# Head of the tensor queue, the order of the first nine pairs, and the partitions of one add, in an attention and mixture-of-experts kernel

## The chip, the cores and the metric

The kernel runs on one core of a Trainium2 chip. Times are device microseconds of that core; the kernel's time is the median of several executions, and one further execution was recorded by the hardware profiler.

## What is computed

Two attentions follow each other. The first has 8 batches of 8 heads over 576 positions of width 64, with a bias from a running sum. Its output, 8 batches of 576 rows of 512, goes through four experts, each a one-head attention of its own with projections in and out; a gate picks two experts per row.

```python
scores = scale * np.matmul(q, k.transpose(0, 1, 3, 2))
cum = np.cumsum(np.maximum(s, 0.0), axis=-1)
bias = -(cum[:, :, :, None] - cum[:, :, None, :])
scores = np.where(causal, -1e9, scores + np.minimum(bias, 0.0))
attn = softmax(scores)                      # less the row maximum, sum + 1e-9
x = np.matmul(attn, v)                      # heads side by side: B, S, 512
logits = x @ w_gate                         # the two largest of four weigh the experts
for e in range(4):                          # causal softmax attention per expert
    a = softmax(where(causal, -1e9, scale * (x @ wq[e]) @ (x @ wk[e]).T))
    out += gate[e] * (a @ (x @ wv[e])) @ wo[e]
```

## The kernel before, in words

The unit of work is a pair of heads, or of experts. Fifty pairs follow each other: pairs 0 to 7 are the heads of the first two batches, 8 and 9 the experts of batch 0, then four head pairs and two expert pairs by turns. Each of the five engines works through its own queue in the order in which the program issues to it. That order is written out by hand in the string `STEPS`: a step `n:x` issues the step x of slot n, and each engine takes its steps in the order of the string. Slots begin at -2, since a pair's preparation begins two slots ahead. The steps used below are these.

- `h0` to `h3` (ScalarE) round the queries and keys of pair n+2 to their high parts; `hc` (a DMA) brings its running sums; `l0`, `l1` and on (VectorE, on GpSimd for pair 1) form the low parts of pair n+1, and `lq`, `lk` copy its high parts.
- `m0` to `m5` (TensorE) form products whose row maximum is wanted, `m0` to `m2` for pair n+2 and `m3` to `m5` for pair n+1, each in a PSUM bank; `M0` to `M5` (VectorE) reduce a bank and give it back. `mt` (TensorE) turns the maxima of pair n+1 from columns into rows, `mA` (ScalarE) negates and `mq` (two DMAs) writes them beside the queries. All this stands ahead of the pair's scores.
- `s0` to `s6` (TensorE, lines 674 and 679) are the scores of pair n, each in a bank; `E0` to `E6` (ScalarE, line 695) take the exponent and give the bank back; `d0` to `d3` (GpSimd) clear the triangle and add the row sums up in the tile `r` (`d1` at lines 755 and 756, `d3` at line 766).
- `v0` to `v7` (TensorE, line 832) multiply by the values of pair n-1, `V0` and `V1` copy out. `n0`, `n1` (VectorE, line 949) scale two pairs by the reciprocal sums, which `r0` to `r4` bring through DMAs; `N` and `o` split the result in high and low parts.
- `ld` (a DMA) loads queries and keys of pair n+3 into one of three `raw` tiles; `lv` loads values; `w` loads weights, into the tiles that the reciprocals use too.
- `z0` to `z47` (TensorE, line 1273) are dummy products of 64 columns that put TensorE to work between others; ahead of all stands a loop of `FIRST_IDLE` dummy products. Each shows as two records in the trace.

A bank is taken by a step on TensorE from the one given back longest ago, so the order of steps also sets whose release a product waits for. With eight banks, in the order before `10:s5` takes the bank that `10:M4` gives back, and on VectorE `10:M4` stands right behind `9:n0`. From slot 10 on the string is the same in both orders, and seven of its lines in slots 6 to 8 are too.

Of the kernel before, what the change touches and what calls it, by code (L numbers as in the profile page):

```python
# [40 lines left out]
FIRST_IDLE, IDLE = 12, 48  # L41
# [28 lines left out]
def heads(t, at, c0, c1):  # L70
# [17 lines left out]
    "-2:h3 -1:lq -2:h1 -1:lk -2:z0 -2:z1 -2:z2 -2:h0 -2:z3 -1:l1 0:lq -2:z4 -2:z5 -1:ld -2:hc -2:z6 "  # L88
    "-1:cu -2:h2 -2:m1 -1:m5 -1:h0 -1:l0 -2:m2 -2:z7 -1:f1 -1:h3 0:h2 0:h0 -2:M1 -2:M2 -2:z8 -2:z9 "
    "0:f2 -1:hc -1:m3 -1:h2 -1:M5 -2:m0 -1:h1 0:hc -2:z10 -2:z11 -1:M3 0:h3 -1:m4 0:m4 -2:M0 -1:M4 "  # L90
    "-1:m0 -1:M0 -1:m2 -1:M2 -2:z12 -1:mt -1:mA -1:mq -2:z13 0:h1 -1:m1 -1:M1 0:m5 0:m3 0:M5 0:m0 "
    "-2:z14 -2:z15 -2:z16 -2:z17 -2:z18 0:l0 0:lk 0:s4 0:E4 0:M4 0:s2 0:M3 0:s1 0:E1 0:s5 0:l1 0:mt "
    "0:mA 0:s6 0:M0 0:ld 0:s3 0:s0 0:E5 -2:z19 0:m2 1:l0 0:E2 0:mq 0:E3 0:E0 1:m3 1:m4 -2:z20 -2:z21 "
    "-2:z22 1:hc 1:h2 1:h3 0:d1 0:d0 1:lq 0:E6 0:m1 1:m5 1:M3 1:M5 -2:z23 0:d3 1:h1 1:s5 1:s3 1:E3 "
    "1:s4 1:h0 0:M1 1:s1 1:s2 1:s0 1:E5 0:M2 1:s6 0:lv 1:E2 -2:z24 1:ld 1:v3 1:E4 0:d2 1:d2 1:v4 1:M4 "
    "2:m3 0:e0 2:lq 1:lk 1:E1 1:E0 1:m0 1:M0 0:lc -2:z25 1:v5 1:v6 -2:z26 1:mt 1:lv 1:mA 2:M3 2:h0 "
    "2:lv 1:l1 -2:z27 2:m4 1:m2 1:M2 2:m5 1:m1 1:v7 1:V1 -2:z28 -2:z29 0:b0 1:mq 0:B0 1:v0 1:v1 1:d1 "
    "2:M5 1:v2 2:M4 1:M1 2:lk -2:z30 2:h3 -2:z31 1:d0 2:h2 1:e0 2:hc 2:s1 2:E1 2:s6 2:E6 2:d3 2:mt "
    "2:l0 2:s3 2:mA 2:ld 2:s5 2:h1 2:s2 2:s0 1:E6 2:E3 2:E2 2:s4 2:E4 3:h2 2:v0 2:l1 3:l0 -2:z32 "
    "-2:z33 1:w0 2:m2 3:m5 2:E5 1:d3 3:M5 2:v1 -2:z34 -2:z35 2:M2 2:v2 2:V0 -2:z36 2:E0 2:w0 -2:z37 "  # L100
    "1:b0 3:m3 -2:z38 3:m4 1:B0 3:ld 3:M3 2:m1 1:V0 3:h1 2:v3 2:v4 2:v5 2:mq 2:v6 2:M1 3:h0 2:v7 3:w0 "
    "2:V1 2:m0 3:s1 3:s0 3:hc 3:E1 2:d0 3:h3 3:s6 3:E6 3:s2 3:r0 3:E0 2:M0 2:d1 3:M4 3:s4 3:s3 3:s5 "
    "3:mt -2:z39 2:d2 2:e0 4:m3 3:lk 3:d0 4:m5 -2:z40 -2:z41 -2:z42 -2:z43 3:r1 4:M5 -2:z44 3:E5 "
    "-2:z45 3:m2 3:E2 4:m4 3:E3 4:w1 4:h3 3:d1 3:E4 3:d3 4:M3 3:e0 4:h0 3:M2 3:d2 -2:z46 3:v0 3:v1 "
    "3:v2 3:m0 2:b0 3:b0 3:mA 4:lk 2:B0 4:M4 3:l1 3:r2 4:lv 3:V0 3:r4 3:m1 3:v3 3:v4 3:lq 4:l0 3:B0 "
    "4:h1 3:n1 4:h2 3:v5 3:mq 3:v6 3:v7 3:M1 4:s1 4:E1 4:hc 3:r3 4:s0 4:E0 3:n0 5:r0 4:s5 4:s3 4:E3 "
    "3:M0 4:s2 4:s4 4:d0 4:E5 4:mt 4:mA -2:z47 5:r1 4:s6 4:l1 4:E6 5:m5 4:E2 3:lv 4:m0 -2:zz 5:m4 "
    "4:M0 4:m2 4:v3 3:V1 4:m1 4:E4 5:w0 4:w0 4:d1 4:v4 4:v5 4:ld 4:v6 4:M2 4:v7 4:lq 4:V1 3:N1 5:r2 "
    "4:e0 5:h1 4:v0 4:v1 5:v3 5:v4 5:h0 4:v2 5:v0 5:v1 4:d2 4:d3 5:v2 5:M5 5:m3 5:hc 4:V0 5:M4 5:h2 "
    "5:M3 4:mq 5:s6 5:r3 5:s0 5:h3 5:V0 5:E6 5:s5 3:N0 5:s3 3:o1 4:M1 3:o0 5:s2 5:s4 5:E3 5:s1 5:E0 "  # L110
    "5:r4 5:E4 7:ld 5:E1 5:mt 5:n0 5:lq 6:m5 5:E5 5:v5 5:v6 5:n1 5:v7 5:m1 5:mA 5:m2 6:m4 5:N0 5:V1 "
# [9 lines left out]
    "8:E3 8:n0 8:l1 8:s0 8:s4 8:mt 8:g1 8:g2 8:g3 8:E2 8:s6 8:mA 9:l0 8:h2 8:ld 7:d2 8:a0 8:E0 8:hc "  # L121
    "7:d3 8:a1 7:v5 8:v3 8:A1 7:v6 7:v2 8:N0 8:A0 8:s1 8:E4 8:l2 8:E1 8:s5 8:E5 9:t0 9:T0 9:m3 9:h2 "
    "9:l2 8:d0 9:h0 9:m5 7:v7 8:v0 8:v1 8:v4 8:v5 8:v6 8:mq 8:m0 9:r0 9:M3 9:r1 9:r2 9:m4 9:M5 8:m2 "
    "9:h3 8:d1 7:V0 8:m1 9:lk 8:E6 8:v7 8:e0 8:M0 8:V1 8:v2 9:s0 9:s5 8:V0 9:s1 8:M1 9:h1 8:d2 9:s2 "
    "9:E0 7:V1 8:M2 9:M4 9:t1 9:s4 9:hc 9:s3 9:mt 9:E5 9:s6 9:E1 9:E4 8:o0 8:N1 9:mA 9:E3 9:l1 10:m5 "
    "9:v0 9:E2 9:v1 9:v2 9:V0 9:E6 9:m1 9:m2 9:r4 10:h2 9:d0 9:lq 9:n1 9:m0 9:r3 8:d3 10:M5 10:lq "
    "9:l3 10:m4 10:m3 9:n0 9:mq 9:T1 9:td 10:h0 9:d1 10:v0 10:v1 9:v3 10:M4 9:v4 10:V0 9:v5 9:v6 9:v7 "
    "10:lv 9:N0 10:ld 9:V1 9:M0 10:s2 10:s5 10:s3 8:o1 10:E2 9:o0 10:E5 10:s0 9:N1 10:E3 10:s4 10:s6 "
    "9:M1 10:s1 9:o1 10:M3 9:d2 10:E4 10:p2 9:M2 10:h3 10:P2 10:p0 10:p1 10:h1 10:mt 10:lk 10:E0 "
    "10:l2 10:E1 10:l3 9:d3 10:hc 10:a1 10:a0 10:d1 10:P0 10:A1 10:d2 10:mA 10:A0 10:d0 10:m0 11:hc "  # L130
    "11:lk 10:l1 10:m2 11:m3 10:m1 10:l0 11:m4 10:v2 10:v3 10:v4 10:v5 11:h3 10:M2 11:r0 10:P1 10:mq "
# [1250 lines left out]
```

## Time and profile before

| | us |
|---|---|
| median of 3 runs | 663.42 (662.9 to 664.12) |
| the profiled execution | 663.8 |
| its span on the core | 662.1 |
| TensorE busy | 650.7 |
| VectorE busy | 558.2 |
| ScalarE busy | 450.3 |
| GpSimd busy | 424.4 |

The span runs from the first to the last instruction; 1.7 us of the profiled time lie around it. TensorE counts as busy while a dummy product runs, and while it runs at half clock; the granted clock is shown apart.

### The profile page before, as it was taken

To read this page: it belongs to the slowest core of one execution; us is meant where nothing else is said; L and a number is where in the kernel's file an instruction comes from. 1 tells how busy PE (TensorE), PEld (TensorE's weight loads), DVE (VectorE), ACT (ScalarE), POOL (GpSimd) and SP (SyncE) were. 2 spreads that over 40 slices of the span, in tenths; PEclk is the share of its full clock that TensorE was granted. 3 is DMA by queue.
4 is the path that set the end of the run, shared out by engine and by line. 5 is a ranking of instruction groups with operands and counts; after the bars stand their busy time and mean duration, and the time that the engine had idled before them with its cause. 6 is when DMAs were issued, how large, how long until landed. Compare 5 with 4: busy or idle time off the path is not lost.

```text
span 662.1 us, 16453 instructions
## 1 busy us (share of the span) xinstructions
PE 650.7 (98%) x5976; PEld 547.3 (83%) x5976; DVE 558.2 (84%) x1432; ACT 450.3 (68%) x980; POOL 424.4 (64%) x530
## 2 busy tenths in 40 slices
PE   8999999999999999999999999999999999999997
PEld 5888798888897888888888878978888889779885
DVE  8687978997989889898989989897998986781995
ACT  5488867766668766776667776677676757556464
POOL 8576566678667576667776586585766765837030
PEclk8699999989999999999999999999999999999999
DMA  4253552553554463535633545445535443331323
GB/s 145 64 165 113 163 140 64 143 143 92 154 141 119 130 165 82 139 121 151 176 93 110 174 119 158 128 123 142 158 84 142 139 120 97 99 106 37 93 65 111
DMA packets 52286, 81.22 MB, mean 123 GB/s; under 512 B 18430, under 2 KB 26622, under 8 KB 52206
## 3 DMA queue, kind: packets, MB, share of 16 engines
q1 hardware_dynamic: 52206, 80.18, 44.5%
q8 instruction: 47, 0.77, 0.5%
q14 instruction: 33, 0.27, 0.1%
HBM read 44.55 MB, written 10.09 MB: 83 GB/s over the span
## 4 chain that ended last, share of the span: by engine, by line
PE 81%; DVE 7%; DMA 4%; ACT 3%; issue 2%; SPq 1%; DVEq 0%; ACTq 0%
PE pvp L832 16%; PE pq L1058 12%; PE s L674 11%; PE s L679 10%; PE pw L1058 9%; PE mx L613 9%; PE po L1058 7%; PE sm L882 3%; DVE mx L627 3%; PE idle L1273 1%; DMA rb<-rr 1%; ACT p L695 1%; DVE pv L949 1%; DMA raw<-in_qk_dram 1%; PE po L1034 1%
## 5 line engine op out<-in xcount | busy, mean ns | idle before, releaser
L627 DVE CUSTOM_DVE_ANT_0 mx<-mx,mask 128x64 f32<-128x64 f32 (+7 forms) x432 | 185.0, 445 | 38.9 <-PE mx L613 24.5
L695 ACT ACTIVATE p<-s 128x512 f32<-128x512 f32 x288 | 161.5, 593 | 64.3 <-PE s L679 63.3
L715 POOL TENSOR_SCALAR_AFFINE_SELECT p<-p 64x128 f32<-64x128 f32 (+2 forms) x183 | 111.7, 611 | 117.8 <-ACT p L695 103.2
L674 PE MATMUL s<-q,k 128*128 128x320 f32 (+3 forms) x672 | 173.5, 288 | 2.3 <-DVE mcol L627 2.2
L679 PE MATMUL s<-q,k 97*128 97x320 f32 (+3 forms) x672 | 163.8, 285 | 0.6 <-DMA q<-mr 0.6
L674 PEld LDWEIGHTS s<-q,k 128*128 128x128 f32 (+1 forms) x672 | 125.4, 187 | 8.3 <-issue 1.9
L679 PEld LDWEIGHTS s<-q,k 97*128 97x128 f32 (+1 forms) x672 | 124.6, 187 | 2.2 <-DMA q<-mr 1.0
L761 POOL TENSOR_TENSOR r<-r,p 128x640 f32<-128x640 f32 x84 | 118.0, 1405 | 6.8
L587 DVE TENSOR_TENSOR q<-raw,q 64x576 fp32r<-64x576 f32 (+1 forms) x86 | 82.8, 971 | 25.7 <-ACT q L547 11.9
L832 PE MATMUL pvp<-p,v 128*64 128x192 f32 (+4 forms) x1024 | 102.2, 334 | 0.8 <-DVE mcol L627 0.8
L613 PE MATMUL mx<-k,q 96*64 96x448 bf16 (+6 forms) x960 | 92.6, 300 | 1.8 <-DMA k<-p 0.9
L832 PEld LDWEIGHTS pvp<-p,v 128*64 128x64 f32 x1024 | 66.8, 136 | 28.4 <-ACT p L695 2.5
L592 DVE TENSOR_TENSOR k<-raw,k 64x576 fp32r<-64x576 f32 (+1 forms) x86 | 87.1, 1020 | 2.6 <-ACT k L578 0.3
L1058 PE MATMUL pq<-xh,wqkh 128*128 128x288 f32 x256 | 77.7, 304 | 0.3 <-ACT pv L846 0.3
L1058 PE MATMUL pq<-xl,wqkh 128*128 128x288 f32 x256 | 75.5, 295 | 0.0
L1058 PE MATMUL pq<-xh,wqkl 128*128 128x288 f32 x256 | 75.5, 295 | 0.0
L550 ACT ACTIVATE k<-raw 64x576 fp32r<-64x576 f32 x96 | 64.6, 681 | 7.5 <-DMA raw<-in_qk_dram 5.7
L613 PEld LDWEIGHTS <-q 96*64 96x64 bf16 x960 | 46.6, 111 | 27.0 <-issue 10.0
L627 DVE DVE_READ_ACCUMULATOR2_ANT mcol<- 128x1 f32 x480 | 65.9, 137 | 0.7
L547 ACT ACTIVATE q<-raw 64x576 fp32r<-64x576 f32 x96 | 64.2, 678 | 1.1
L755 POOL TENSOR_TENSOR r<-p 128x256 f32<-128x256 f32 x37 | 28.9, 780 | 52.6 <-ACT p L695 52.1
L846 ACT ACTIVATE pv<-pvp 128x320 f32<-128x320 f32 (+1 forms) x92 | 36.4, 405 | 27.5 <-PE pvp L832 27.4
(151 smaller groups left out, 1249.3 us busy)
## 6 DMA issues: line engine op xcount, KB each, us to landing
raw<-in_qk_dram SPq DMA_DIRECT2D x30, 576.0 KB
rb<-rr SPq DMA_DIRECT2D x92, 144.0 KB
q<-q SPq DMA_DIRECT2D x45, 288.0 KB
k<-k SPq DMA_DIRECT2D x39, 288.0 KB
v<-in_vm_dram SPq DMA_DIRECT2D x32, 256.0 KB
out_dram<-o SPq DMA_DIRECT2D x32, 256.0 KB
q<-mr SPq DMA_DIRECT2D x96, 2.2 KB
raw<-in_qk_dram SPq DMA_DIRECT2D x4, 288.0 KB
```

The lines of the kernel that those rows point to most:

```text
L550: nc.scalar.activation(k2[0:64, j], get_raw(n, j)[64:128], AF.Copy)
L587: eng.tensor_tensor(a[64:128, j], get_raw(n, j)[0:64], q2[0:64, j].bitcast(F32), op=OP.subtract)
L592: eng.tensor_tensor(c[0:64, j], get_raw(n, j)[64:128], c[64:128, j].bitcast(F32), op=OP.subtract)
L613: nc.tensor.matmul(t[64 * j : 64 * j + 64, c0 : c0 + k1 - k0], q2[0:RC, 64 * qt : 64 * qt + 64], k2[0:RC, k0:k1], start=True, stop=True,)
L627: nc.vector.tensor_tensor_reduce(t[:, c0 : c0 + w], t[:, c0 : c0 + w], mask[:, m0 : m0 + w], scale=1.0, scalar=mcol[n][:, 9:10] if slot == ...
L674: nc.tensor.matmul(t[0:nk, c0 : c0 + q1 - q0], K1[r1(n)][:, j, k0 : k0 + nk], Q1[r1(n)][:, j, q0:q1], start=True, stop=False,)
L679: nc.tensor.matmul(t[0:nk, c0 : c0 + q1 - q0], K2[r2(n)][0 : RM + 1, j, k0 : k0 + nk], Q2[r2(n)][0 : RM + 1, j, q0:q1], start=False, stop= ...
L695: nc.scalar.activation(heads(ptile[n], PCHUNK[ci], 0, 512)[:, x % 2], tl[x], AF.Exp, scale=0.125)
L715: nc.gpsimd.affine_select(out=a, in_=a, pattern=[[0, a.shape[1]], [1, w]], compare_op=OP.is_ge, fill=0.0, base=0, channel_multiplier=-1,)
L761: add(r[:, :, q0:S], r[:, :, q0:S], chunk_of(2, c, c + S - q0), op=OP.add)
L832: nc.tensor.matmul(cur[h][64 * j : 64 * j + 64, q0 - PVC[h] : q1 - PVC[h]], vsl(j, kt), heads(ptile[n], at, c, c + q1 - q0)[:, j], start=f ...
L1058: nc.tensor.matmul(t[0:nk, 0:w], l, r, start=(x == 0), stop=(x == len(terms) - 1))
```

## The change

1. The loop at the head issues 32 dummy products of 128 columns in place of 12 of 256.
2. The steps of slots -2 to 6 and of slots 8 to 10 are put in another order. No step is added or left out, 779 places of the string lie between the first and the last that differ.
3. In the last step of a pair's sums, `d3`, the add on GpSimd takes 128 partitions in place of 64; the triangle is still cleared in 64. The other 64 rows of its second operand hold zeros.

The diff, with the lines of `STEPS` cut to the parts spoken of below:

```diff
-FIRST_IDLE, IDLE = 12, 48
+FIRST_IDLE, IDLE = 32, 48
...
-    "-2:h3 -1:lq -2:h1 -1:lk -2:z0 -2:z1 -2:z2 -2:h0 -2:z3 -1:l1 0:lq -2:z4 -2:z5 -1:ld -2:hc -2:z6 "
-    "-1:cu -2:h2 -2:m1 -1:m5 -1:h0 -1:l0 -2:m2 -2:z7 -1:f1 -1:h3 0:h2 0:h0 -2:M1 -2:M2 -2:z8 -2:z9 "
-    "0:f2 -1:hc -1:m3 -1:h2 -1:M5 -2:m0 -1:h1 0:hc -2:z10 -2:z11 -1:M3 0:h3 -1:m4 0:m4 -2:M0 -1:M4 "
-    "-1:m0 -1:M0 -1:m2 -1:M2 -2:z12 -1:mt -1:mA -1:mq -2:z13 0:h1 -1:m1 -1:M1 0:m5 0:m3 0:M5 0:m0 "
-    "-2:z14 -2:z15 -2:z16 -2:z17 -2:z18 0:l0 0:lk 0:s4 0:E4 0:M4 0:s2 0:M3 0:s1 0:E1 0:s5 0:l1 0:mt "
-    "0:mA 0:s6 0:M0 0:ld 0:s3 0:s0 0:E5 -2:z19 0:m2 1:l0 0:E2 0:mq 0:E3 0:E0 1:m3 1:m4 -2:z20 -2:z21 "
-    "-2:z22 1:hc 1:h2 1:h3 0:d1 0:d0 1:lq 0:E6 0:m1 1:m5 1:M3 1:M5 -2:z23 0:d3 1:h1 1:s5 1:s3 1:E3 "
...
-    "4:M0 4:m2 4:v3 3:V1 4:m1 4:E4 5:w0 4:w0 4:d1 4:v4 4:v5 4:ld 4:v6 4:M2 4:v7 4:lq 4:V1 3:N1 5:r2 "
...
+    "-1:ld -2:h0 -2:h3 -2:z0 -2:hc -2:h2 -1:h0 -2:z1 -1:l0 -2:h1 -1:lk -1:l1 -2:z2 -2:z3 -2:z4 -1:lq "
+    "-1:m3 0:h2 0:lk -1:M3 -2:m0 0:lq -2:m2 -1:h2 -1:h1 -2:m1 -1:m5 -1:m4 -2:M0 -2:z5 -2:z6 -2:z7 "
+    "-1:cu -1:f1 -1:h3 -2:z8 -2:z9 -2:z10 -2:M1 -2:z11 0:h0 -2:z12 -2:z13 -2:z14 -1:hc 0:m4 0:f2 "
+    "-1:m1 -1:m2 -2:M2 -1:M5 -1:M4 0:h1 -1:mt -1:mA -2:z15 -1:M1 0:m3 0:h3 0:hc 0:m5 0:M3 -2:z16 "
+    "-1:m0 0:M5 1:m4 0:m2 -2:z17 -2:z18 -1:M0 -1:mq 0:s0 0:E0 -1:M2 0:ld 0:s4 0:E4 0:s3 0:E3 0:s1 "
+    "0:l1 0:l0 -2:z19 0:M4 0:M2 0:s6 0:mt 0:mA 0:E1 0:s2 0:mq 0:E2 0:s5 0:E6 1:m5 0:E5 0:m1 1:M5 1:h3 "
+    "0:m0 1:h2 1:m3 1:hc 0:d1 1:M3 0:lv -2:z20 -2:z21 -2:z22 -2:z23 2:lv 1:s0 1:E0 1:s6 1:s5 1:M4 "
+    "1:E6 0:M1 1:s1 0:M0 1:s2 1:h1 1:s3 1:ld 0:d3 0:d0 1:h0 1:E1 1:E2 1:s4 1:mt 2:m5 2:hc 1:m1 1:v0 "
+    "1:l0 1:E4 2:M5 0:d2 2:lq 1:v1 0:e0 -2:z24 -2:z25 1:mA -2:z26 -2:z27 1:E3 1:m2 -2:z28 1:lk 2:h0 "
...
+    "4:s3 4:s4 4:E1 4:E2 4:s5 4:s0 4:E3 4:lq 4:lk 4:mt 4:s6 4:l1 4:m1 4:E5 3:o1 5:lv 5:m5 4:E0 4:E6 "
+    "4:ld 4:mA 5:r0 5:r1 4:m2 3:N0 4:E4 5:m4 5:M5 5:m3 4:M2 4:v0 4:v3 4:v1 4:v2 5:M3 4:v4 5:h1 4:v5 "
+    "5:h2 5:v3 5:M4 4:w0 4:d0 5:r2 4:v6 5:v0 4:M1 4:v7 5:v1 4:d1 5:v4 4:e0 4:V1 7:ld 4:d2 5:v2 5:V0 "
...
-    "9:v0 9:E2 9:v1 9:v2 9:V0 9:E6 9:m1 9:m2 9:r4 10:h2 9:d0 9:lq 9:n1 9:m0 9:r3 8:d3 10:M5 10:lq "
-    "9:l3 10:m4 10:m3 9:n0 9:mq 9:T1 9:td 10:h0 9:d1 10:v0 10:v1 9:v3 10:M4 9:v4 10:V0 9:v5 9:v6 9:v7 "
-    "10:lv 9:N0 10:ld 9:V1 9:M0 10:s2 10:s5 10:s3 8:o1 10:E2 9:o0 10:E5 10:s0 9:N1 10:E3 10:s4 10:s6 "
+    "9:v4 9:v5 10:m5 9:m1 9:l0 9:n0 9:r4 9:v6 9:T1 10:h1 9:v0 9:v1 10:lk 9:E6 8:o1 9:v2 9:N0 10:M5 "
+    "10:v0 10:hc 9:E4 9:E5 10:v1 8:e0 9:V0 9:v7 9:l3 10:V0 9:E3 10:m4 9:m2 9:d1 9:n1 10:h3 9:V1 10:m3 "
+    "10:M3 9:d2 9:M2 9:m0 9:N1 9:o0 9:o1 9:mq 9:d3 10:s0 10:s4 10:E4 10:lq 10:s2 10:lv 10:E2 10:E0 "
+    "10:M4 10:s1 10:E1 9:M1 10:s3 10:p2 10:h2 10:p1 10:p0 9:M0 10:ld 10:h0 10:E3 10:s5 10:l2 10:E5 "
...
-                a = heads(p, PTAIL, 0, 64)[0:64]
-                lower(a, 64)
+                a = heads(p, PTAIL, 0, 64)
+                lower(a[0:64], 64)
                 if n >= SUMMED:
-                    nc.gpsimd.tensor_tensor(r[0:64, :, 512:S], r[0:64, :, 512:S], a, op=OP.add)
+                    nc.gpsimd.tensor_tensor(r[:, :, 512:S], r[:, :, 512:S], a, op=OP.add)
...
     for k in range(FIRST_IDLE):
-        idle(0, 256)
+        idle(0, 128)
```

## Rows read from the trace of the kernel before

**Rows 1.** The page, part 1: busy time, share and instructions of each engine.
```profile
PE 650.7 (98%) x5976; PEld 547.3 (83%) x5976; DVE 558.2 (84%) x1432; ACT 450.3 (68%) x980; POOL 424.4 (64%) x530
```

**Rows 2.** Windows: stretch, length, busy (count) PE, PEld, DVE, ACT, POOL; PEclk, DMA share, GB/s.
```profile
84.60:139.40 54.80, 54.80 (x526) 47.43 (x526) 46.66 (x123) 39.35 (x88) 38.58 (x40) 1.00 0.47 120
139.40:146.00 6.60, 5.05 (x29) 4.88 (x29) 6.53 (x14) 3.66 (x7) 5.65 (x6) 0.74 0.72 177
...
200.00:300.00 100.00, 99.68 (x935) 83.23 (x928) 90.40 (x235) 71.95 (x157) 71.52 (x86) 1.00 0.47 129
```

**Rows 3.** Windows, short ones around the changes of the granted clock.
```profile
12.20:12.40 0.20, 0.20 (x9) 0.16 (x4) 0.00 (x0) 0.20 (x1) 0.20 (x1) 0.82 0.99 219
...
29.40:29.60 0.20, 0.20 (x3) 0.19 (x2) 0.19 (x1) 0.03 (x1) 0.20 (x1) 1.00 0.00 0
...
142.00:143.00 1.00, 1.00 (x6) 1.00 (x5) 0.96 (x5) 0.69 (x2) 0.92 (x2) 0.52 0.77 200
```

**Rows 4.** Timeline of the first 30 us, dummy products: start, us, engine, line.
```profile
4.95 0.23 PEld L1273 LDWEIGHTS idle<-p 128*64 128x64 f32 x1 [0.20 <-issue]
5.37 3.25 PEld L1273 LDWEIGHTS idle<-p 128*64 128x64 f32 x15 [0.20 <-issue]
...
9.06 0.33 PE L1273 MATMUL idle<-p 128*64 128x64 f32 x2
...
10.31 0.33 PE L1273 MATMUL idle<-p 128*64 128x64 f32 x2
...
20.54 0.45 PE L1273 MATMUL idle<-p 128*64 128x64 f32 x2
...
22.57 0.48 PE L1273 MATMUL idle<-p 128*64 128x64 f32 x2
```

**Rows 5.** The chain that ended last, first 62 us: start, length, what.
```profile
9.95 1.89 DMA k<-p
...
18.41 0.31 PE mt L647
...
23.05 0.57 PE s L674
...
29.53 0.19 PE idle L1273 x2
29.73 0.80 PE mx L613 x8
```

**Rows 6.** Waits of VectorE, first 85 us: total, times, longest.
```profile
DVE q L587 <- ACT p L695: 5.6, 1, 5.6
```

**Rows 7.** The chain that ended last, 60 to 150 us.
```profile
70.02 6.94 DMA raw<-in_qk_dram
```

**Rows 8.** TensorE's timelines: start, us; in brackets the idle time before.
```profile
77.62 0.42 PE L613 MATMUL mx<-k,q 96*64 96x512 bf16 x2 [0.66 <-DVE mcol L627]
...
84.58 0.40 PE L1058 MATMUL pq<-xh,wqkh 128*128 128x288 f32 x1 [0.29 <-ACT pv L846]
...
141.65 0.41 PE L674 MATMUL s<-q,k 128*128 128x320 f32 x1 [1.55 <-DVE mcol L627]
```

**Rows 9.** Timeline of all engines, 124 to 152 us, the lines from 137.7 us.
```profile
137.75 3.12 DVE L949 TENSOR_TENSOR pv<-pv,rb 128x576 f32<-128x576 f32 x1
...
138.00 0.71 POOL L755 TENSOR_TENSOR r<-p 128x256 f32<-128x256 f32 x1
...
138.68 0.99 POOL L756 TENSOR_TENSOR r<-p 128x384 f32<-128x384 f32 x1
...
139.63 0.63 POOL L715 TENSOR_SCALAR_AFFINE_SELECT p<-p 128x512 f32<-128x512 f32 x1
```

**Rows 10.** Line 949: durations ns min/median/max, first and last start.
```profile
L949 DVE TENSOR_TENSOR pv<-pv,rb x46: 695/759/3120, 67.0 to 627.5; 128x576 f32<-128x576 f32 x46
```

**Rows 11.** GpSimd's groups by shape: busy us, mean ns, idle before.
```profile
L756 POOL TENSOR_TENSOR r<-p 128x384 f32<-128x384 f32 x37 | 40.7, 1099 | 0.0
...
L766 POOL TENSOR_TENSOR r<-r,p 64x128 f32<-64x128 f32 x44 | 22.1, 502 | 8.3 <-DVE r L761 4.8
```

49 rows, old and new, of the table STEPS are left out of this document.

## The prediction

> **What bounds the kernel now.** I read the page first, then the kernel by windows, then the stretches in which the windows show something other than a busy TensorE at full clock. The page has TensorE busy for 98% of the span, VectorE for 84%, ScalarE and GpSimd for less [rows 1]. By windows TensorE has no idle time between 84.6 and 139.4 us, and in a stretch from the middle it is busy for 99.7 of 100 us while VectorE is busy for 90 [rows 2]. So the queue of TensorE sets the time: a microsecond that TensorE loses anywhere is not made up for later, and a step on another engine costs something only where TensorE comes to wait for it.
>
> What a new order can give back is therefore the time that TensorE loses in the stretch that is reordered, up to some 146 us. [...] The clock falls to half at about 12.3 us and is full again only from 29.4 us [rows 3]. Two waits of 0.66 and 0.29 us stand at 77 and 84 us [rows 8]. [...]
>
> **The head of the queue.** The first records of the dummy products come 0.42 us apart, and later 3.25/15 = 0.217 us apart [rows 4]: TensorE starts at half clock, and the step to full comes some 4.3 us after its start. The 24 records of 256 columns become 64 of 128. At half clock one takes half of 0.42, so that 20 are done by 5.4 us. The other 44 cost at least half of 0.217 each, 4.8 us in all, and at most what a record of the 64-column dummies takes, (10.31 - 9.06)/8 = 0.156 us, or 6.9 us. Between these I take 0.13, thus 5.7 us, and the head ends at 11.1 us. Five `z` follow at 0.31 each: the first maxima products start at 12.7 us (bounds 11.8 and 13.9). They can't start before the running sums land, 9.95 + 1.89 = 11.84 us [rows 5], so of the longer head only 0.8 us shows.
>
> [...]
>
> **From there to the first scores.** The 20 maxima products of pair 0 now stand together, then ten `z`, then ten products of pair 1, then `mt`. At full clock a product costs 0.8/8 = 0.10 us [rows 5] and a `z` 0.31: 2.0 + 3.1 + 1.0 = 6.1, so `mt` comes at 18.8 us, where it was at 18.41 [rows 5]. At half clock a `z` costs (22.57 - 20.54)/4 = 0.51 [rows 4] and a product 0.20. Behind `mt` TensorE has 16 products and four `z` ahead of the first score: 2.8 us at full clock, 5.2 at half. In the trace 4.6 us lie between `mt` and the first score [rows 5], in which the negated maxima also travel through ScalarE and two DMAs. Pair 0's scores take 29.53 - 23.05 = 6.5 us at half clock, 3.3 at full, and one more `z` stands among them. So the scores end
>
> - with a full clock throughout: 18.8 + 4.6 + 0.3 + 3.3 = 27.0 us, 2.5 before those of the trace;
> - with half from `mt` on: 18.8 + 5.2 + 0.5 + 6.5 = 31.0, 1.5 later;
> - with half from the first of the ten `z`, 14.7 us: 5.1 + 2.0 to `mt`, 5.2, 0.5 and 6.5 more, 34.0 us, 4.5 later.
>
> I take the middle one. The clock fell after a run of `z` with gaps [rows 3, 4], and ten of them in a row are such a run; but dense products now stand on either side of it.
>
> **VectorE behind the scores.** VectorE loses 5.6 us once in `l0` of pair 2, which has to await the end of pair 0's scores since it overwrites their operand [rows 6]; six reductions queue up behind it. In the new order these six stand ahead of it. Five of them have their products behind the same scores, so the wait stays, but pair 2's maxima are ready sooner. Next late is then ScalarE, whose exponents and copies of pair 1 stand in one row. I give back 1.5 us of the 5.6 (bounds 0 and 3). The start together comes to 1.5 - 1.5 = 0, within -5.5 and +4.5.
>
> **The load of pair 7.** The chain has a transfer of 6.94 us into `raw`, issued at 70.02 [rows 7]. It is `4:ld`, which on SyncE's queue stood behind the weights `5:w0` and `4:w0`; these write to tiles that the reciprocals have first to give back. Now `4:ld` stands ahead of both. The two waits that follow, 0.95 us together, can go altogether or not at all, as both end on other engines; I take half, -0.5. The weights are late instead, but their first product is beyond 84 us.
>
> **The stall at 140 us.** In slots 9 and 10 one add of `n0` on VectorE takes 3.12 us, where the median of 46 is 0.76 [rows 9, 10]: 2.36 too long. `10:M4` is behind it in the queue, and with it the bank for which `10:s5` waits 1.55 us [rows 8]. The half clock then costs half of 3.4 us, so the stall is worth 1.55 + 1.7 = 3.25 us. In the new order the scores take a bank from a reduction first at `10:s1`, behind three other blocks of scores in place of one, and `9:n0` stands further ahead. Of the 3.25 I take 2.5 as gone, keeping 0.7 for new waits in an order that has not run here; bounds 0 and 3.25.
>
> GpSimd was in three instructions without a gap from 138.00 to 140.26 us [rows 9], as long as the excess. [...]
>
> **The tail's add.** An add of 384 elements over 128 partitions takes 1099 ns, 366 per 128 elements; `d3`'s 128 elements over 64 partitions take 502 [rows 11]. The number of partitions shows no price, so I take 0. If it doubled, 44 times 0.5 us would be 22 us on an engine that idles for a third of the span [rows 1]. That cover is missing for the last two pairs alone, 1 us at most. A gain is excluded in the middle, where TensorE has no wait to lose [rows 2].
>
> **Sum.** 0 - 0.5 - 2.5 + 0 = -3.0 us. The profiled execution took 663.8 us (span 662.1 and 1.7 around it), so 660.8; the median of the runs lies 0.4 lower, which makes 660.4.
>
> **Rivals.** *The ten `z` bring the clock down (slower).* It is at half from the first of them, by 15 us, and the scores end 4.5 us late; nothing of VectorE's part comes back, since everything waits for the scores. +4.5 - 0.5 - 2.5 = +1.5, some 664.9. For it: the fall at 12.3 us behind `z` [rows 3, 4]. Against: the denser head directly before. It decides if the fall comes ahead of `mt` by over 3 us. Chance 0.15.
>
> *The stall at 140 us comes back*, by the meeting of adds on VectorE and GpSimd: `9:n1` now stands right behind `9:d1` in the string, and `10:M3`, whose bank `10:s1` needs, right behind `9:n1`. With the whole 3.25 us lost as now: -0.5, some 662.9. Against: one add in 46 was that long [rows 10]. Chance 0.17.
>
> *The clock holds throughout the start.* -2.5 - 1.5 there and -3.0 for the rest give -7.0, some 656.4, if TensorE's queue stays full between 30 and 84 us. VectorE, busy for 46.7 of 54.8 us behind that [rows 2], would follow. Chance 0.13. The forecast keeps 0.55.
>
> **Chances and range.** About 0.2%, 1.3 us, is what a measurement here can tell from no change. Of the forecast 0.52 lies on the faster side beyond it and 0.03 within; of the second rival 0.02, 0.12 and 0.03 (faster, within, slower, the last if a wait is added); of the first 0.02 within and 0.13 slower; the third is faster. That makes 0.67 faster, 0.17 the same, 0.16 slower. The forecast's own range is 658.5 to 662.3. From 657 to 665 about half of the first and of the third rival are left out, and nothing else.
>
> **What would show it.** Right: the head ends at about 11 us and the first maxima products start by 13; `mt` lies at 18 to 20 us; the granted clock falls once between 15 and 23 us; no add of line 949 is over 2 us; the clock stays full from 84 to 150 us, and slot 10's scores come some 2 to 3 us earlier. Wrong: half clock from 15 us until behind 31; a new wait of TensorE for a bank in slots 3 to 6 or 8 to 10; or an earlier start that is lost again before 84 us to ScalarE's row of exponents. From slot 11 on both orders should run alike, shifted.

## The result, and the profile after

The changed kernel takes 655.93 us (median of 4 runs, 653.07 to 656.22), the kernel before 663.16 beside it: a ratio of 0.988, interval 0.985 to 0.991. It is faster, as forecast, but by 7.2 us where 3.0 were forecast, and the time lies below the range of 657 to 665. The profiled execution took 656.09 us with a span of 654.3. The page's busy times and the clock's line of its 40 slices:

```profile
PE 643.5 (98%) x6016; PEld 545.6 (83%) x6016; DVE 553.0 (85%) x1432; ACT 449.4 (69%) x980; POOL 423.7 (65%) x530
...
PEclk9999999999999999999999999999999999999999
```

TensorE is the bound as in [rows 1]: its busy time fell by 7.2 us and its share stayed. The 40 added records are the head's. What changed is seen in windows of the changed kernel (columns as in [rows 2]):

```profile
10.00:15.00 5.00, 4.14 (x37) 2.94 (x35) 4.29 (x9) 4.89 (x8) 4.85 (x6) 1.00 0.44 97
15.00:20.00 5.00, 4.51 (x46) 3.40 (x45) 4.72 (x21) 1.54 (x4) 4.84 (x3) 1.00 0.01 3
...
25.00:30.00 5.00, 4.71 (x42) 4.12 (x37) 4.87 (x17) 3.92 (x8) 4.86 (x11) 1.00 0.44 117
...
139.00:146.00 7.00, 7.00 (x75) 5.71 (x75) 6.80 (x17) 4.03 (x11) 6.75 (x8) 1.00 0.23 51
200.00:300.00 100.00, 100.00 (x946) 84.15 (x946) 88.47 (x230) 71.94 (x157) 68.44 (x87) 1.00 0.52 139
634.00:640.00 6.00, 6.00 (x49) 3.98 (x47) 4.43 (x8) 2.30 (x8) 0.07 (x1) 0.72 0.00 0
```

The reader is to see four things. The granted clock is 1.00 in each window where [rows 3] has it fall at 12.3 us and rise again at 29.4. The stall of [rows 2] at 139.4 to 146 us is gone. The middle, where [rows 2] had 99.68 busy of 100, has 100.00. And there is a new half-clock stretch at 636 to 639 us, with TensorE at work throughout. TensorE's timeline of the start shows how the first two came about:

```profile
1.05 9.06 PE L1273 MATMUL idle<-p 128*64 128x128 f32 x66 [1.05 <-DVE p L345]
...
11.90 0.39 PE L613 MATMUL mx<-k,q 96*64 96x512 bf16 x1 [0.55 <-DMA k<-p]
12.60 1.46 PE L613 MATMUL mx<-k,q 96*64 96x512 bf16 x19 [0.31 <-DMA k<-p]
...
18.34 0.28 PE L647 MATMUL mt<-p,mcol 128*9 128x128 f32 x1 [0.49 <-DVE mcol L627]
...
20.71 0.41 PE L674 MATMUL s<-q,k 128*128 128x320 f32 x1
```

The head and the first `z` end by 10.1 us (the prediction had 11.1 for the head alone), the maxima start at 11.9 and 12.6 us (12.7), `mt` comes at 18.34 (18.8). Behind `mt` prediction and trace part: the first score follows `mt` by 2.4 us, not 4.6 as in [rows 5], and the scores of pair 0 end at 24.5 us, where the chosen case had 31.0 and the case of a full clock 27.0. The two costliest causes of TensorE's waits over the whole span (total, times, longest; `q<-mr` is the DMA `mq` of the negated maxima, `mcol` the column of maxima that a reduction writes before it gives its bank back):

```profile
PE s L679 <- DMA q<-mr: 1.5, 2, 1.2
PE mx L613 <- DVE mcol L627: 1.5, 1, 1.5
```

Four places that both kernels reach in the same order give the account, in us of the profiled executions (`pq` holds the experts' projections of queries and keys):

| reached | before | after | earlier by |
|---|---|---|---|
| first product into `pq` [rows 8] | 84.58 | 78.23 | 6.35 |
| a product of slot 10's sums (`sm`) | 151.07 | 142.90 | 8.17 |
| one such product thirty pairs later | 535.03 | 524.58 | 10.45 |
| first of the last products (line 1034) | 650.55 | 642.81 | 7.74 |

So the start gives 6.3 us, slots 6 to 10 another 1.8, the middle 2.3 although its order is untouched, and the end takes 2.7 back: 1.2 us for the wait on `q<-mr` and half of the 3.4 us at half clock.

### The profile page after: what moved, and what is told of

The parts are those of the page before. It is cut to its first block, busy times and chain, and to the rows that moved or that the text cites. A ratio compares the mean times of both kernels' runs of the same rounds, so it can differ in the third digit from the quotient of the medians.

```text
span 654.3 us, 16533 instructions
## 1 busy us (share of the span) xinstructions
PE 643.5 (98%) x6016; PEld 545.6 (83%) x6016; DVE 553.0 (85%) x1432; ACT 449.4 (69%) x980; POOL 423.7 (65%) x530
## 4 chain that ended last, share of the span: by engine, by line
PE 89%; DVE 4%; DMA 3%; ACT 2%; SPq 1%; issue 1%; DVEq 0%; ACTq 0%
PE pvp L832 19%; PE pq L1058 15%; PE s L674 11%; PE s L679 11%; PE mx L613 9%; PE pw L1058 8%; PE po L1058 7%; PE sm L882 4%; DVE mx L627 1%; PE po L1034 1%; PE mt L647 1%; PE idle L1273 1%; DMA q<-mr 1%; SPq L924 1%; PE gt L1152 1%
## 5 line engine op out<-in xcount | busy, mean ns | idle before, releaser
L715 POOL TENSOR_SCALAR_AFFINE_SELECT p<-p 64x128 f32<-64x128 f32 (+2 forms) x183 | 107.0, 586 | 123.4 <-ACT p L695 101.0
L674 PE MATMUL s<-q,k 128*128 128x320 f32 (+3 forms) x672 | 169.2, 283 | 0.6 <-DVE mcol L627 0.3
L679 PE MATMUL s<-q,k 97*128 97x320 f32 (+3 forms) x672 | 160.2, 281 | 1.5 <-DMA q<-mr 1.5
L674 PEld LDWEIGHTS s<-q,k 128*128 128x128 f32 (+1 forms) x672 | 122.5, 182 | 6.3 <-issue 1.9
L679 PEld LDWEIGHTS s<-q,k 97*128 97x128 f32 (+1 forms) x672 | 121.6, 182 | 3.0 <-DMA q<-mr 1.9
L587 DVE TENSOR_TENSOR q<-raw,q 64x576 fp32r<-64x576 f32 (+1 forms) x86 | 83.6, 979 | 20.0 <-ACT q L547 11.9
L613 PE MATMUL mx<-k,q 96*64 96x448 bf16 (+6 forms) x960 | 90.5, 294 | 2.5 <-DVE mcol L627 1.5
L846 ACT ACTIVATE pv<-pvp 128x256 f32<-128x256 f32 (+1 forms) x92 | 36.5, 405 | 30.0 <-PE pvp L832 29.8
```

The source lines that it names most:

```text
L587: eng.tensor_tensor(a[64:128, j], get_raw(n, j)[0:64], q2[0:64, j].bitcast(F32), op=OP.subtract)
L613: nc.tensor.matmul(t[64 * j : 64 * j + 64, c0 : c0 + k1 - k0], q2[0:RC, 64 * qt : 64 * qt + 64], k2[0:RC, k0:k1], start=True, stop=True,)
L674: nc.tensor.matmul(t[0:nk, c0 : c0 + q1 - q0], K1[r1(n)][:, j, k0 : k0 + nk], Q1[r1(n)][:, j, q0:q1], start=True, stop=False,)
L679: nc.tensor.matmul(t[0:nk, c0 : c0 + q1 - q0], K2[r2(n)][0 : RM + 1, j, k0 : k0 + nk], Q2[r2(n)][0 : RM + 1, j, q0:q1], start=False, stop= ...
L715: nc.gpsimd.affine_select(out=a, in_=a, pattern=[[0, a.shape[1]], [1, w]], compare_op=OP.is_ge, fill=0.0, base=0, channel_multiplier=-1,)
```

## The experiments

All kernels of one set ran on one chip, beside the kernel before. That kernel's own runs spread from 658.5 to 667.6 us, mostly with the mean granted clock (0.978 to 0.991 over the run). So what is compared are ratios over all runs, each with its 95% interval, and landmarks of the traces.

**Set 1: each part of the change alone, put into the kernel before.** The new head alone:

```diff
-FIRST_IDLE, IDLE = 12, 48
+FIRST_IDLE, IDLE = 32, 48
-        idle(0, 256)
+        idle(0, 128)
```

> The kernel before with the new head alone: 32 dummy products of 128 columns in place of 12 of 256. If the head is what holds TensorE's clock at full through the start, the granted clock stays 1.00 from 5 to 30 us, pair 0's scores end at 25 to 27 us in place of 29.5, and 3 to 5 us are gained. If it is the new order that holds the clock, the clock falls once more at 12 to 16 us and the time is within 1 us of the kernel before.

Measured: 664.12 us, ratio 1.002 (0.999 to 1.005). The new order of slots -2 to 6 alone, with the old head:

```diff
-    "-2:h3 -1:lq -2:h1 -1:lk -2:z0 -2:z1 ...
+    "-1:ld -2:h0 -2:h3 -2:z0 -2:hc -2:h2 ...   (500 steps, to 6:v2)
```

> The kernel before with the new order in slots -2 to 6 alone; old head, old order in slots 8 to 10, old add. If the head holds the clock, it falls at 12 to 16 us, the ten dummies in a row run at half clock, and at most 1.5 us are gained, or up to 4 lost. If the order does it, 5 to 6.5 us are gained and the clock stays at full.

Measured: 660.25 us, ratio 0.997 (0.994 to 1.000). The new order of slots 8 to 10 alone:

```diff
-    "8:n0 8:l1 8:s0 8:s4 ... 10:m0
+    "8:ld 7:d2 7:d3 8:n0 ... 9:td
```

> The kernel before with the new order in slots 8 to 10 alone. By the two traces the gain grows by 1.6 to 1.8 us between 85 and 151 us, so 1.6 to 2 us if these slots alone bring it, with no wait of 1.55 us and no half clock at 140 us but perhaps one wait of 1.5 us at about 125. If the long add of line 949 comes from the meeting of instructions and not from the order, it is there again and the time is within 0.7 us of before.

Measured: 664.31 us, ratio 1.002 (0.999 to 1.005). The add on 128 partitions alone:

```diff
-                a = heads(p, PTAIL, 0, 64)[0:64]
-                lower(a, 64)
+                a = heads(p, PTAIL, 0, 64)
+                lower(a[0:64], 64)
-                    nc.gpsimd.tensor_tensor(r[0:64, :, 512:S], r[0:64, :, 512:S], a, op=OP.add)
+                    nc.gpsimd.tensor_tensor(r[:, :, 512:S], r[:, :, 512:S], a, op=OP.add)
```

> The kernel before with the add over 128 partitions alone. If its partitions have no price, within 0.7 us of before and the add's mean at 0.50 to 0.52 us. The rival: the gain of some 2 us that the new kernel makes between 200 and 500 us, where the order is the same, comes from this add; then 1.5 to 2.5 us are gained here.

Measured: 659.75 us, ratio 0.997 (0.993 to 1.000). No part has the gain by itself, and none of the intervals leaves 1 clearly. Windows of the first two, the new head above and the new order below, show why the start gave nothing:

```profile
12.00:14.00 2.00, 1.64 (x17) 1.27 (x16) 1.30 (x6) 1.98 (x4) 1.96 (x3) 1.00 0.79 176
14.00:16.00 2.00, 2.00 (x14) 1.29 (x14) 1.93 (x9) 0.40 (x1) 1.86 (x3) 0.54 0.29 64
```

```profile
10.00:12.00 2.00, 0.33 (x1) 0.16 (x2) 1.97 (x2) 1.95 (x4) 1.95 (x2) 0.89 0.03 7
12.00:14.00 2.00, 1.91 (x17) 1.26 (x16) 1.17 (x4) 1.93 (x3) 1.96 (x3) 0.50 0.80 176
```

In the old order the clock falls at 14.2 us even behind the dense head; in the new order behind the old head it falls at 11.6. There TensorE had nothing to do for two microseconds ahead of the maxima (its timeline):

```profile
11.67 1.65 PE L614 MATMUL mx<-k,q 96*64 96x512 bf16 x6 [2.03 <-DMA k<-p]
```

**Set 2: what holds the clock.** New head and new order of the start together, slots 8 to 10 and the add as before (the two diffs of above):

> The kernel before with the new head and the new order of slots -2 to 6; slots 8 to 10 and the tail's add as before. Theory 1: the gain is the start's, and it takes head and order together, since each alone let the clock fall at 12 to 14 us. Then the granted clock is 1.00 from 0 to 50 us, the first product into pq starts at 78 to 79 us where it was at 84.6, and the ratio is 0.989 to 0.992; at 140 us the wait of 1.5 us and the half clock may or may not stand. Theory 2: slots 8 to 10 and the add have a part in the gain; then the ratio stays above 0.994 although the clock holds. Theory 3: the clock's hold in the changed kernel was an accident of that run; then it falls here before 20 us and the ratio is 0.997 to 1.002.

Measured: 657.40 us, ratio 0.991 (0.988 to 0.994); the first product into `pq` at 78.08. Its windows:

```profile
12.00:14.00 2.00, 2.00 (x24) 1.31 (x24) 1.36 (x4) 1.95 (x4) 1.96 (x3) 1.00 0.73 164
14.00:16.00 2.00, 2.00 (x14) 1.60 (x14) 1.93 (x10) 1.01 (x2) 1.86 (x3) 1.00 0.34 74
```

The stall of before stands in this trace too, with a wait of 1.7 us and a half clock from 136 us on. With the runs of set 1 this is a square of four: old or new head by old or new order. In the profiles the clock holds in one corner only. The runs are less sharp: all five of this kernel have a mean granted clock of 0.996 or more, none of the kernel before is over 0.991, but those with the new head and the old order have 0.980 to 0.995, and one of the ten with the new order and the old head has 0.999 and took 654.85 us. So the new order uses a clock that holds, and the new head makes it hold in nearly every run: in sets 3 and 4 the kernels with this head, this start and dummies of 64 columns have 5 of 49 runs at 0.988 to 0.991 (659.3 to 661.1 us), the others at 0.994 or more. The kernel before with wider dummies between the steps, nothing else:

```diff
-    def idle(k, cols=64):
+    def idle(k, cols=128):
```

> The kernel before, with each of the 48 dummy products between the steps 128 columns wide in place of 64; head and order as before. At full clock a record of 128 columns takes 8.79/66 = 0.133 us in the head, one of 64 columns 0.13 to 0.16, so that the wider ones cost next to nothing. Theory 1a: what let the clock fall at 12.3 us is the run of narrow dummies around the first maxima products. Then the clock holds or falls clearly later than 12.3 us, the first product into pq starts 3 to 6 us earlier, and the ratio is 0.990 to 0.996. Theory 1b: what let it fall are the two waits of 0.46 us there, which stay. Then it falls at 12 to 13 us again and the ratio is 0.998 to 1.002 (slower, if the wide dummies cost double at half clock: 38 of them by 0.2 us give up to 1.010).

Measured: 658.39 us, ratio 0.993 (0.991 to 0.995). The clock holds:

```profile
10.00:15.00 5.00, 4.82 (x37) 2.97 (x36) 4.22 (x11) 4.20 (x7) 4.85 (x5) 1.00 0.42 94
15.00:20.00 5.00, 3.94 (x39) 2.51 (x37) 4.86 (x22) 1.80 (x4) 2.89 (x2) 1.00 0.03 7
```

That is theory 1a's result, but the run doesn't exclude the short waits as the cause. The wider dummies end later and so shorten them too: of the two of 0.46 us ahead of the maxima one is gone and the other is 0.18. Against the waits as the only cause speaks a longer one ahead of `mt`, through which the clock holds. TensorE's timeline:

```profile
12.36 0.76 PE L613 MATMUL mx<-k,q 96*64 96x384 bf16 x11 [0.18 <-DMA k<-p]
...
17.86 0.28 PE L647 MATMUL mt<-p,mcol 128*9 128x128 f32 x1 [1.06 <-DVE mcol L627]
```

Yet the first product into `pq` comes only 2.1 us earlier (82.48): TensorE now waits 1.3, 0.8, 0.6 and 0.3 us between 60 and 160 us, for `q<-mr`, `xl`, a bank and `q<-q`. With the old order a full clock runs into the other engines; the new order has one wait of 0.2 us between 30 and 90 us. The changed kernel with a head of few long products that ends at the same time:

```diff
-FIRST_IDLE, IDLE = 32, 48
+FIRST_IDLE, IDLE = 16, 48
-        idle(0, 128)
+        idle(0, 256)
```

> The changed kernel with a head of 16 dummy products of 256 columns in place of 32 of 128. Twelve of them with two more records end at 8.3 us, four more add 8 records of 0.217, so that this head ends at 10.1 us as the changed kernel's does. Theory 1b: only the length of the head counts, since it closes the gap of 2 us ahead of the first maxima products that stood behind the old head in the new order. Then the clock is 1.00 throughout the start and the time that of the changed kernel, ratio 0.987 to 0.991. Rival: the many short products of the new head do it (their weight loads keep TensorE at work twice as often). Then the clock falls at 12 to 14 us and the ratio is 0.995 to 0.999.

Measured: 654.87 us, ratio 0.988 (0.983 to 0.994), clock 1.00 throughout the start: what the head does is to last until 10 us. Its grain shows no part, though one of the four runs has a mean clock of only 0.988 (658.45 us). And the changed kernel with narrower dummies between the steps:

```diff
-    def idle(k, cols=64):
+    def idle(k, cols=32):
```

> The changed kernel with the 48 dummy products between the steps 32 columns wide in place of 64. Theory 1a: the width of the dummies counts for the clock. Ten of them in a row stand at 14 to 17 us; halved, they let the clock fall between 13 and 20 us, the scores of pair 0 end 4 to 6 us later, and the ratio to the kernel before is 0.995 to 0.999. Theory 1b: only waits count. The narrower dummies end a little sooner and leave at most short waits of the same length; the clock holds, ratio 0.986 to 0.991.

Measured: 659.04 us, ratio 0.995 (0.992 to 0.998). The clock falls in the profile, although that is of the fastest of the ten runs (the mean clocks are 0.978 to 0.994):

```profile
15.00:18.00 3.00, 2.17 (x22) 1.64 (x23) 2.75 (x13) 1.21 (x4) 2.86 (x4) 0.98 0.01 5
18.00:22.00 4.00, 4.00 (x27) 3.26 (x23) 3.79 (x17) 0.55 (x1) 3.93 (x2) 0.50 0.29 71
```

The wait ahead of `mt` grew as well, from 0.49 to 0.83 us, as the narrow dummies end sooner. The fall at 17.9 us put the first product into `pq` 2.5 us back, to 80.74. This start falls behind waits of 0.24 and 0.83 us with dummies of 32 columns; the old order with 128 held through 0.18 and 1.06. So the length of the waits alone doesn't decide. How much is the dummies' width and how much the waits that it moves, no run separates. Halving the width is enough to lose the hold of the changed kernel.

**Set 3: the wait at 123 us, and the add from the other side.** In all four profiles so far with the new order of slots 8 to 10 one step stalls. Timelines of VectorE, GpSimd and TensorE in the changed kernel:

```profile
120.74 1.78 DVE L587 TENSOR_TENSOR q<-raw,q 64x576 fp32r<-64x576 f32 x1
...
120.63 1.27 POOL L753 TENSOR_TENSOR r<-p 128x512 f32<-128x512 f32 x1
121.86 1.15 POOL L715 TENSOR_SCALAR_AFFINE_SELECT p<-p 128x512 f32<-128x512 f32 x1
...
123.58 0.64 PE L613 MATMUL mx<-k,q 96*64 96x512 bf16 x4 [1.47 <-DVE mcol L627]
```

The subtraction takes 1.78 us where the median is 0.75, ends 0.6 us behind GpSimd's sum, which started 0.1 us ahead of it, and the reductions behind it release TensorE's bank 1.5 us late. The step moved behind them:

```diff
-    ... 8:mA 8:E2 9:l2 7:v6 9:lq ...  8:v4 8:M0 8:mq ...
+    ... 8:mA 8:E2 7:v6 9:lq ...  8:v4 8:M0 9:l2 8:mq ...
```

> The changed kernel with one step moved: 9:l2, the subtraction of line 587, stands behind 8:M0 in place of ahead of 7:v6. In all four profiles with the new order of slots 8 to 10 it took 1.78 us where the median is 0.75, beside three instructions of GpSimd without a gap, and TensorE's maxima product behind it waited 1.5 us for the bank of the reduction queued behind it. Theory 4, the meeting of the two engines is the cause: the reductions, whose form of 512 columns never took over 0.76 us, run ahead of the step, the wait of 1.5 us near 123 us is gone, and from the sum at 114.6 us to the one at 142.9 us the path takes 26.8 us in place of 28.3; the ratio is 0.984 to 0.988. Rival: GpSimd's row blocks whichever instruction stands there; the reductions are late by as much, and the stretch stays at 28 us or over, ratio as that of the changed kernel.

Measured: 652.51 us, ratio 0.987 (0.984 to 0.990). The wait is gone, the stretch from 113.66 to 140.69 us takes 27.0 us where it took 28.3, and the step, which now starts 0.05 us ahead of GpSimd's next sum, has its usual time:

```profile
121.57 0.75 DVE L588 TENSOR_TENSOR q<-raw,q 64x576 fp32r<-64x576 f32 x1
```

This is the fastest version found, 1.4 us by medians below the changed kernel on the same chip, though the two intervals overlap. The same with the head of 16 long products and dummies of 128 columns:

> The version before this one (9:l2 moved), with a head of 16 products of 256 columns and dummy products of 128 columns between the steps. Theory 1a: wide dummies cost next to nothing at full clock and make the hold at the start certain in each run; then the granted clock of the runs is 0.994 or more in each, their scatter narrower than the changed kernel's, and the ratio is 0.982 to 0.987. Rival: the clock holds in the changed kernel anyway, and the wider dummies cost what their columns take, up to 38 by 0.1 = 4 us, so that the ratio is 0.989 or above.

Measured: 655.50 us, ratio 0.991 (0.988 to 0.994): the rival held. Its first product into `pq` is at 80.33, 3.0 us behind that of the version above; where the clock holds already, wide dummies cost what they take. The changed kernel with the old add (set 1's last diff, turned round):

> The changed kernel with the tail's add on 64 partitions as before. From the sum at 142.9 us to that at 524.6 us the changed kernel and the two runs made from it take 381.3 to 381.7 us, all kernels made from the old one 383.1 to 384.4, though the order of the steps is the same there. Theory 5: the add on 128 partitions has the 2 us, by ending together with other work of GpSimd or VectorE; then the stretch takes 383 us or more here. Rival: the two new orders together have them, as VectorE enters the stretch with more lead; then it takes 381.3 to 381.8 here too, and the time is that of the changed kernel within 0.3%.

Measured: 657.30 us, ratio 0.994 (0.992 to 0.996). The stretch from 143.19 to 528.08 us takes 384.9 us. Theory 5 held: beside both new orders the add carries the two microseconds of the middle. The changed kernel once more, for the comparison:

> The changed kernel itself once more, on the chip of the other runs of this call. Theory 1: its clock holds through the start in nearly each run, so that its granted clock is 0.993 or more in most, and the ratio is 0.986 to 0.990 again. Rival (theory 3, the hold was luck): some of its runs show 0.98 to 0.99 and a time of 659 to 663 us, and the ratio is 0.990 to 0.995.

Measured: 653.88 us, ratio 0.989 (0.986 to 0.992), a granted clock of 0.996 or more in all six runs. Putting the old add back costs 3.4 us. At the first place where the two part, the same steps stand on both engines; timelines of VectorE and GpSimd with the old add, and TensorE's line behind:

```profile
141.75 3.67 DVE L592 TENSOR_TENSOR k<-raw,k 64x576 fp32r<-64x576 f32 x2
145.43 2.01 DVE L587 TENSOR_TENSOR q<-raw,q 64x576 fp32r<-64x576 f32 x1
...
141.19 0.84 POOL L766 TENSOR_TENSOR r<-r,p 64x128 f32<-64x128 f32 x1
142.00 0.72 POOL L755 TENSOR_TENSOR r<-p 128x256 f32<-128x256 f32 x1
142.70 1.00 POOL L756 TENSOR_TENSOR r<-p 128x384 f32<-128x384 f32 x1
...
148.47 0.33 PE L613 MATMUL mx<-k,q 96*64 96x256 bf16 x4 [0.77 <-DVE mcol L627]
```

and in the changed kernel's second profile:

```profile
141.09 2.12 DVE L592 TENSOR_TENSOR k<-raw,k 64x576 fp32r<-64x576 f32 x2
143.22 1.47 DVE L587 TENSOR_TENSOR q<-raw,q 64x576 fp32r<-64x576 f32 x1
...
140.54 0.85 POOL L766 TENSOR_TENSOR r<-r,p 128x128 f32<-128x128 f32 x1
141.35 1.25 POOL L755 TENSOR_TENSOR r<-p 128x256 f32<-128x256 f32 x1
142.56 1.52 POOL L756 TENSOR_TENSOR r<-p 128x384 f32<-128x384 f32 x1
```

The add itself takes the same time. But behind the add on 64 partitions GpSimd goes on (0.72, 1.00, its usual times) and VectorE's three subtractions take 5.7 us; behind the add on 128 VectorE goes first, they take 3.6, and GpSimd's sums are stretched to 1.25 and 1.52 instead. GpSimd can spare it, VectorE can't: TensorE waits 0.77 us for a bank.

This is no single case. Take every place where a VectorE operation with two inputs starts while such an add runs, and GpSimd's next instruction follows the add without a gap. In the profiles of this document without an extra write behind the add (set 4 has two with one), VectorE then ended 2.3 to 2.8 us behind the add in all 16 cases with 64 partitions, so GpSimd had gone first, and 0.6 us behind it in all 15 with 128. Beside the changed kernel's second profile the old add loses 1.6, 0.5, 0.5 and 0.7 us in four stretches between 143 and 401 us.

**Set 4: what the add does, and whether slots 8 to 10 help beside it.** The changed kernel with slots 8 to 10 in the old order:

> The changed kernel with slots 8 to 10 in the old order (new head, new order of slots -2 to 6, new add). Theory 6: the new order of slots 8 to 10 gives nothing and costs its own wait of 1.5 us at 123 us, while the stall at 140 us goes by the add. Then this kernel is not slower than the changed one: ratio 0.984 to 0.989, no wait of TensorE over 1 us between 80 and 150 us. Rival: the new order is worth the 2.5 us of the prediction, and the old one brings them back; then the stall near 133 to 140 us stands again (a wait of 1.5 us or more) and the ratio is 0.990 to 0.994.

Measured: 654.52 us, ratio 0.991 (0.987 to 0.994), and no wait of TensorE at all between 80 and 150 us. The ratio fell into the rival's range, but what the rival rests on, the stall at 133 to 140 us, isn't there; and another kernel of this set that differs from the changed one by a hidden 0.1 us has the same ratio (the last one below). Beside the new add neither order of these slots is measurably better. In the traces the path from the first product into `pq` to slot 10's sums takes 63.1 us here and 64.7 in the changed kernel, which is the 1.5 us that theory 6 gave to the new order's own wait. Then the old add with a small write behind it:

```diff
                     nc.gpsimd.tensor_tensor(r[0:64, :, 512:S], r[0:64, :, 512:S], a, op=OP.add)
+                    nc.gpsimd.memset(nudge, 0.0)      # 1 x 8 values
```

> The changed kernel with the add on 64 partitions, and behind each of the 44 adds a write of eight values on one partition, some 0.1 us of GpSimd that nothing waits for. Theory 7: the add's form acts only through the order in which VectorE and GpSimd come to their common work: 0.1 us more on GpSimd lets VectorE go first, as the add on 128 partitions did at 141.8 us. Then the waits of 0.5 to 1.5 us between 143 and 400 us change places or go, and the time leaves that of the kernel with the old add (ratio 0.9942) by over 1 us, more likely downwards: 0.988 to 0.992. Rival: 64 partitions are dear as such (the form holds VectorE up); then the time stays, 0.993 to 0.996.

Measured: 658.06 us, ratio 0.995 (0.993 to 0.998). And the same write behind the new add:

> The changed kernel with the same write of some 0.1 us behind each add, the add on 128 partitions. Theory 7: it moves the meetings here too; new waits of 0.5 to 1.5 us appear between 143 and 525 us, and the ratio is 0.990 to 0.995. Rival, the form alone counts: 44 times 0.1 us of an engine with spare time is hidden, and the ratio is that of the changed kernel, 0.986 to 0.990.

Measured: 654.68 us, ratio 0.991 (0.988 to 0.994). The write took 95 ns, 44 times. Theory 7 fell: a shift of 0.1 us moves nothing that shows. With it VectorE's two subtractions of line 592 take 3.74 us behind the add on 64 partitions and 2.12 behind that on 128, as without it, and the new add's kernel got no new wait; its ratio is 0.001 above the range that the rival set, far inside its interval. So the form of the add decides who goes next, and not a moment of 0.1 us.

## Why the prediction was wrong

**The step that failed** is the choice of the middle case for the start: "with half from `mt` on ... I take the middle one". The clock held through the start (1.00 in each window from 10 to 30 us), which the prediction had as its third rival with 0.13 and priced at 656.4; the measured time is 0.5 below that. That this price came so close is luck: the rival had 4.0 us for the start and 3.0 for the rest, where the traces have 6.3 and 1.4 (1.8 and 2.3 gained, 2.7 lost at the end). The ground for a fall, a run of dummies with gaps in [rows 3, 4], fits the runs as far as they go: narrower dummies bring the fall back, wider ones keep it away in the old order, and both move the waits as well. What was missed is that head and order had been changed at once. The head of 11 us, of which "only 0.8 us shows", was costed as a delay; its use is to close the gap of 2 us that the new order would otherwise have ahead of its first product. What the 20 maxima in one row add to that, no run shows apart. Head or order alone gives a ratio of 1.002 or 0.997, both together 0.991.

**The start in numbers.** Of its 0 us (bounds -5.5 and +4.5) 6.3 were measured, below the bound. Maxima and `mt` came within 0.8 us of the working. The head ended 1.3 us ahead of it, at 9.8: its records step from 0.21 to 0.11 us apart at 4.4 us, where the working had 5.4 and 0.13. The granted clock reads 1.00 on both sides of that step (0 to 5 and 5 to 10 us, before and after), so the working's half clock there is an estimate from the spacing alone. The 4.6 us from `mt` to the first score were taken over from a trace at half clock into the case of a full one; they are 2.4, near the 2.8 that the working had for TensorE's queue alone. VectorE's 5.6 us [rows 6] are gone altogether, its longest wait for TensorE's maxima is 1.6; 1.5 were given back for it. The wider dummies in the old order show that clock and order need each other: 2.1 us by the clock alone, 0.3 by the order alone (`pq` at 84.24), 6.5 by head and order together.

**The load of pair 7** (-0.5): its transfer is no longer in the chain between 55 and 90 us and both waits of [rows 8] are gone, so the direction was right. No run separates it from the rest of the start.

**The stall at 140 us** (-2.5 for the new order). Its price of 3.25 us has 1.7 for the half clock; the 3.4 us that this is half of follow from [rows 2], where a mean of 0.74 over 6.60 us is half clock for 52% of it. Up to slot 10's sums 1.8 us came back, so the size was near, but what the stall hung on was missed. With head and start new, the path from the first product into `pq` to these sums falls from 66.4 us to 64.7 by the new order alone (the old add, set 3) and to 63.1 by the new add alone (set 4); with both it is 64.7. So either takes this stall away. The new order moves the steps that meet there, and has a stall of its own; the add of line 766, a term that the prediction had at 0, changes which engine goes first where they meet. The long add of [rows 9] started while one of 64 partitions ran on GpSimd, and ended 0.6 us behind the last of the three instructions that followed. GpSimd's timeline before, and line 949 with the new add alone and in the changed kernel:

```profile
137.13 0.90 POOL L766 TENSOR_TENSOR r<-r,p 64x128 f32<-64x128 f32 x1
```

```profile
L949 DVE TENSOR_TENSOR pv<-pv,rb x46: 694/759/1491, 67.2 to 625.0; 128x576 f32<-128x576 f32 x46
...
L949 DVE TENSOR_TENSOR pv<-pv,rb x46: 694/759/1553, 62.2 to 617.8; 128x576 f32<-128x576 f32 x46
```

Each of the eight profiles with the add on 64 partitions has an add of line 949 of 2.55 to 3.12 us; in the nine with 128 the longest is 1.19 to 1.55, in the old order and in the new. In the kernel before, too, the new add alone leaves nothing of the stall in the trace: the same path takes 63.1 us where it took 66.5. "One add in 46 was that long" misread [rows 10], which show the longest alone: the kernel before has two more, of 2.57 us at 393 and 2.46 at 471 us. The new order of slots 8 to 10 alone is worth +0.2% with an interval around nothing; it has waits of its own, 1.5 us at 129 us and, behind the old add, 0.8 at 153. The second rival's ground, VectorE and GpSimd meeting, fits the runs: the long add goes with line 766's form, and a stall came back elsewhere, at 123 us. Both times VectorE ended 0.6 us behind the GpSimd instructions beside it (140.87 to 140.26 us, 122.52 to 121.90). Which engine goes first is not told by the starts alone. At 123 us it was the one that started first: GpSimd where it was 0.1 us ahead, VectorE where, with the step moved, it was 0.05 ahead. But in set 3's rows with the old add VectorE's subtractions start at 141.75 us, GpSimd's next sum at 142.00, and GpSimd went first.

**The tail's add** (0). Its duration is as costed, 516 ns a piece after 502 in [rows 11]:

```profile
L766 POOL TENSOR_TENSOR r<-r,p 128x128 f32<-128x128 f32 x44 | 22.7, 516 | 8.3 <-DVE r L761 4.8
```

But "a gain is excluded in the middle, where TensorE has no wait to lose" was wrong. The 99.68 of 100 us in [rows 2] hid short waits: between 160 and 530 us TensorE waited 1.3 us in pieces of 0.2 to 0.4 in the kernel before and 0.3 us in the changed one. The rest of the 2.3 lies in time that shows as busy (382.6 us between the two landmarks before, 381.4 after), and no row tells what it was. And an instruction's own duration is not all that it costs if it decides which engine goes next. The add is worth 0.3% in the kernel before (2.3 us, interval -0.1 to 4.6), by its trace at the stall of 140 us and only 0.5 us in the middle, and 3.4 us by medians in the changed one. So the middle's 2.3 us take the add and the new start together: by the traces head and start alone give 0.4 us there, with the add 2.0.

**The end** was not looked at. The 2.7 us there come from the wait of 1.2 us and the half clock at 636 us. Seven of the seventeen profiles have such a fall at that place, two of them of the kernel before with one part changed. Of the four runs of the changed kernel three have a mean granted clock of 0.996 and take 655.8 to 656.2 us, the fourth 1.000 and 653.07. Whether the clock falls there differs from run to run, and no run here tells why; no kernel was tried that changes the end.

**The sum.** Head and start give 6 us, the add 2.3 to 3.4, slots 8 to 10 nothing that the ratios show with the new add and a loss of 2 with the old (set 3 against set 2), and the end takes 0 to 2.7, from run to run. Open is why the add's partitions decide which engine comes next.

## What to carry to other kernels

Where a granted clock falls at the start, look at what stands ahead of the fall as a whole: here neither the longer head nor the new order held the clock in its profile, and a clock that held gave a third as much in the old order as in the new (2.1 and 6.5 us up to the experts' first projection). A stretch in which the bound engine is busy for 99.7% can still give half a per cent: only 1.0 of the 2.3 us found there had shown as idle time. Cost an edit on a helper engine not by its duration alone: ask whom it makes wait, since a form that takes the same time (502 and 516 ns here) can change who goes next. And look at every instance of a stall before you price it as one place: the longest of 46 had two like it.

## What the runs showed of the hardware that was not expected

- Changing nothing but the width of the dummy products changed whether the clock held, the short waits around them moving with it. In the old order it fell at 12.3 us with 64 columns and held with 128; in the new order it held with 64 and fell at 17.9 us with 32.
- A GpSimd add on 64 or on 128 partitions takes the same half microsecond, but behind the one GpSimd goes next and behind the other VectorE, in all 31 cases where both were ready: three subtractions of VectorE took 5.7 us behind the one, 3.6 behind the other, unmoved by 0.1 us more on GpSimd.
- TensorE went to half clock at 636 us in a stretch in which it shows as busy throughout; what it ran there ahead of the fall were gate products on 4 partitions (2.2 us from 632.6 on) and `pvp` products of 128 columns. The same steps kept their clock in ten of the seventeen profiles.
